# Fillers in the PSUM banks of waiting first-batch matmuls, full-width summary scores, and new transfer times in a static schedule

## The chip, the cores and the metric

The kernel runs on one core of one Trainium2 chip. The metric is the device time of one execution in microseconds (us), lower is better. Ratios are the mean time of one kernel's runs over the mean time of the other's runs of the same rounds, so they are not quite the ratio of the medians quoted beside them. A trace is one execution; times in a trace count from its first instruction, and its span is 1.7 to 2.1 us shorter than the device time.

Engines: PE is TensorE (matmul), PEld its weight loads, DVE VectorE, ACT ScalarE, POOL GpSimd, SP SyncE.

## The reference

A block-sparse attention (4 batches x 8 heads, 768 positions, head size 64) feeds a mixture of 8 dense experts whose weights per token come from eight rounds of row and column normalisation.

```python
k_sum = k.reshape(B, H, nb, 32, D).max(axis=3)          # nb = 24 blocks
v_sum = v.reshape(B, H, nb, 32, D).mean(axis=3)
scores_l = q k^T / 8, kept where |i - j| < 16           # local window
scores_s = q k_sum^T / 8 + log(32)                      # "summary scores"
attn = softmax([scores_l, scores_s]) @ [v, v_sum]       # -> x, 3072 x 512
P = exp(x @ w_gate - max); 8 x: normalise rows, columns
out = sum_e P[:, e] * (relu(x @ w1[e]) @ w2[e])         # F = 1024
```

## The kernel before

Two heads form a pair; there are 16 pairs, four to a batch. The first batch (pairs 0 to 3) is cut into halves of the positions so that PE can start early. Expert 0 is computed from each batch as soon as its x is there (its first matmuls are named `hps`), and its projections are `yps`. After about 130 us experts 1 to 7 follow as a multiplication scheme with seven products instead of eight (`pA`, `pQ`, `pR`, `pY`).

Every instruction belongs to a unit of work with an estimated cost. A list scheduler in the kernel's own Python simulates the engines with these costs and fixes, when the kernel is built, the order of each engine.

```python
def load(key, fn, issue, us, deps=()):          # one HBM load in the schedule
    last[0] = add("POOL", issue, fn, [last[0], *deps])
    last[1] = add("DMA", us, None, [add("RING", 0, None, [last[0]], lag=...), last[1]], 100.0)
    U[key] = add("LAND", 0, None, [last[1]], lag=0.9)
...
load(("v", i), lambda: load_v(i), 1.05, 1.85, ...)      # us: time of the transfer
load("w2", lambda: load_w2(0), 0.85, 5.0)
...
# copies of the 16 rows of v next to each chunk, into V_e ("near rows"), pairs 4 to 11
U["near", i] = add("SP", 2.4, lambda: near_values(i), [U["v", i], ...], prio, lag=3.5)
# values of a pair (named av): need near rows, among others
U["A", i, h] = add("PE", 0.4, lambda h=h: values(i, h), [..., U["near", i]], prio, opens=[buf])
...
# order of PE for the first batch, fixed by hand: T, Q transposes of k, q; v block sums;
# S local scores; s summaries; A values; t transposes to x
plan.follow("PE", "T0 Q0 v0 S0 T1 Q1 s0 S1 T2 Q2 s1 A0 S2 v1 T3 A1 Q3 s2 t0 S3 v2 t1 s3 v3 A2 A3 t2 t3")
# where the plan sees PE wait, it puts a matmul on zeros (named idle) until expert 0's first relu
plan.idle = (0.22, lambda: keep_busy(1), U["rl", 0, 0])
```

Summary scores from pair 4 on, two matmuls on 64 columns of the array, one for each half of the positions:

```python
def summaries_2(i):
    r, ss = i % NB, bank("a", "ss")
    for h in range(2):
        at["ss", i, h] = ss[64 * h:64 * h + 64]
        nc.tensor.matmul(ss[64 * h:64 * h + 64, 0:HS], lhsT=ksT[r][:, 0:64],
                         rhs=qT[r][:, W + h * HS:W + (h + 1) * HS], start=True, stop=True)
```

The softmax here doesn't subtract the row's maximum and nothing guards it: scores larger than these inputs give would overflow.

Of the kernel before, what the change touches and what calls it, by code (L numbers as in the profile page):

```python
# [10 lines left out]
BF16 = mybir.dt.bfloat16  # L11
# [117 lines left out]
def kernel(  # L129
# [10 lines left out]
    nc = tc.nc  # L140

    B, H, S, D = q.shape
# [3 lines left out]
    F = moe_w1.shape[2]  # L146
# [4 lines left out]
    PB = H // 2  # L151
    SCALE = 1.0 / float(D) ** 0.5
    W = 16
# [7 lines left out]
    X_BY_DMA = 12  # L161
    WHOLE = 12

    const = ctx.enter_context(tc.tile_pool(name="const", bufs=1))
# [58 lines left out]
    with tc.manual_schedule():  # L223
# [14 lines left out]
        ks = [attn.tile([128, 1, 32], BF16, name=f"ks{i}") for i in range(NB)]  # L238
        ksT = [attn.tile([128, 128], BF16, name=f"ksT{i}") for i in range(NB)]
        v_x = [attn.tile([128, 2, G, VD], BF16, name=f"vx{i}") for i in range(NQ)]  # L240
# [95 lines left out]
        def key_max_split(i):  # L336
            r = i % NB
            nc.vector.tensor_tensor(out=ksT[r][:, 0:64].rearrange("p (j n) -> p j n", j=2),
                                    in0=ks[r][:].to_broadcast([128, 2, 32]),
                                    in1=own[:].to_broadcast([128, 2, 32]), op=ALU.mult)  # L340
# [7 lines left out]
        def block_sums(i):  # L348
            sv = v_x[i % NQ]
            vs = at["vs", i] = bank("a", "vs")[:, 0:2 * D]  # L350
            for g in range(G):
                nc.tensor.matmul(vs.rearrange("p (j d) -> p j d", j=2), lhsT=m_blk[:, g, :],  # L352
                                 rhs=sv[:, :, g, 0:D], start=(g == 0), stop=(g == G - 1))
# [85 lines left out]
        def summaries(i, h, tag):  # L439
            r = i % NB  # L440
            ss, rhs = bank(tag, "ss"), qT[r][:, W + h * HS:W + (h + 1) * HS]
            at["ss", i, h] = ss
            if i < PB and not h:
                for j in range(2):
                    p = slice(64 * j, 64 * j + 64)
                    nc.tensor.matmul(ss[32 * j:32 * j + 32, 0:HS], lhsT=ks[r][p, 0, :], rhs=rhs[p],
                                     start=True, stop=True)
                return
            nc.tensor.matmul(ss[:, 0:HS], lhsT=ksT[r][:], rhs=rhs, start=True, stop=True)

        def summaries_2(i):
            r, ss = i % NB, bank("a", "ss")
            for h in range(2):
                at["ss", i, h] = ss[64 * h:64 * h + 64]
                nc.tensor.matmul(ss[64 * h:64 * h + 64, 0:HS], lhsT=ksT[r][:, 0:64],  # L455
                                 rhs=qT[r][:, W + h * HS:W + (h + 1) * HS], start=True, stop=True)

# [15 lines left out]
        def scores_h(i, h):  # L473
            sg = at["sg", i, h] = banks2("sg")
            for s in range(HG):
                for j in range(2):
                    score_mm(i, sg[:, j, s * LIVE:(s + 1) * LIVE], j, HG * h + s, 0, LIVE)
            for j in range(2):
                score_mm(i, sg[:, j, HG * LIVE:HG * LIVE + W], j, *((HG, 0, W), (HG - 1, LIVE - W, LIVE))[h])
# [18 lines left out]
        def values_h(i, h):  # L498
            sv, em, es = v_x[i % NQ], E_h[(PB * h + i) % NEH], at.pop(("es", i, h))
            av = at["av", i, h] = bank("a", "av")  # L500

            def mm(p0, p1, cc, j, lhsT, rhs, n=VD, start=False, stop=False):
                o = cc * 2 * VD + j * VD
                nc.tensor.matmul(av[p0:p1, o:o + n], lhsT=lhsT, rhs=rhs, start=start, stop=stop,  # L504
                                 skip_group_check=True)

            for cc in range(HG):
                for j in range(2):
                    mm(0, 128, cc, j, em[:, j, cc, 2 * W:2 * W + 128], sv[:, j, HG * h + cc, :],
                       start=(cc == 0 and j == 0))  # L510
            for cc in range(HG):
                c = HG * h + cc
                for j in range(2):
                    if c + 1 < G:
                        mm(96, 128, cc, j, em[0:32, j, cc + 1, 0:32], sv[0:32, j, c + 1, :])
                    if c > 0:
                        mm(0, 32, cc, j, em[96:128, j, cc - 1 if cc else HG, LIVE:PADL],
                           sv[96:128, j, c - 1, :])
            for cc in range(HG):
                mm(0, 128, cc, 0, es[:, cc, :], V_s[i][0:128 if h else 64], n=2 * VD, stop=True)  # L520
# [82 lines left out]

        def keep_busy(n):

            t = bank("m", "idle")
            for _ in range(n):
                nc.tensor.matmul(t[:], lhsT=zeros[:, 0:128], rhs=zeros[:], start=True, stop=True)

# [7 lines left out]
        nc.vector.memset(zeros, 0.0)  # L617
        keep_busy(9)
        for t in v_x:
# [18 lines left out]
        def constants():  # L638
# [10 lines left out]
            for t in ksT:  # L649
                nc.vector.memset(t[:, 64:128], 0.0)  # L650
            for t, n in ((own, 64), (own_n, 32)):
# [200 lines left out]
        def load_pair(i, parts="kqv"):  # L852
            old = i - NQ
            for c in parts:
                if c == "v":
                    load(("v", i), lambda: load_v(i), 1.05, 1.85,
                         [U.get(("A", old, 1)), U.get(("near", old))])
                elif i < PB and c in "qr":
                    h = "qr".index(c)
                    load(("q", i, h), lambda h=h: load_qk(i, 1, h), 0.65, 0.65)  # L860
                else:
                    z = "kq".index(c)
                    load((c, i), lambda z=z: load_qk(i, z), 0.75 if i < PB else 1.65,
                         1.2 if i < PB else 1.55, [U.get(("tr", old, z)), U.get(("tr", old, 2))])

        def pair_start(i, prio):
# [9 lines left out]
            for z in range(0 if i >= BY_DMA else 1 if i < PB else 2):  # L876
                buf = Buffer("m" if i < PB else "a")
                U["tr", i, z] = add("PE", 0.5 if i < PB else 0.34, lambda z=z: tr(i, z),
                                    [U["kq"[z], i], U["ident"]] + (war_k, war_q)[z]
                                    + [U["tr", i, 0] if z else ahead], prio, opens=[buf])  # L880
                U["kT", i, z] = add({"ACT": 0.8, "DVE": 0.95 if i < PB else 0.56}, 0,
                                    lambda z=z: tr_out(U["kT", i, z].on, i, z), [U["tr", i, z]], prio,
                                    uses=[buf])
            U["ks", i] = add("DVE", 0.95, lambda: key_max(i), [U["kT", i, 0], U.get(("km", o))], prio)
            if i >= PB:
                U["km", i] = add("DVE", 0.23, lambda: key_max_split(i), [U["ks", i]] + war_q[2:], prio)
            buf = Buffer("a")
            U["vs", i] = add("PE", 0.4, lambda: block_sums(i),
                             [U["v", i]] + ([U.get(("A", i - NE, 1)), U["vc", i % NE]] if i >= PB else []), prio + 0.01, opens=[buf])
# [39 lines left out]
        def pair_whole(i, prio):  # L929
# [17 lines left out]
            for h in range(2):  # L947
# [4 lines left out]
            buf = Buffer("a")  # L952
            U["ss", i, 0] = U["ss", i, 1] = add("PE", 0.22, lambda: summaries_2(i),
                                                [U["km", i], U["kT", i, 1], U.get(("A", i - NE, 1))], prio, opens=[buf])
# [66 lines left out]
        U["k", 0] = add({"ACT": 0.8}, 0, cast_k, [U["kf32"]])  # L1021
        U["vf32"] = add("LAND", 0, None, [add("RING", 0, None, [])], lag=5.6)
        U["v", 0] = add({"DVE": 0.6}, 0,
                        lambda: copy(U["v", 0].on, v_x[0][:, :, :, 0:D], v_f32), [U["vf32"]])
        U["ident"] = last[0] = add("POOL", 0.35, ident_constant, [last[0]])
        load_pair(1, "kq")
        U["band"] = last[0] = add("POOL", 0.7, band_constants, [last[0]])
        load_pair(2, "kq")
        load_pair(1, "v")
        load_pair(3, "kq")  # L1030
        load_pair(2, "v")
        load_pair(3, "v")
        for n in range(4):
            load(("w1", n), lambda n=n: load_w1(0, n, 4), 0.85, 1.25)
            if n == 1:
                for i in range(PB):
                    load_pair(i, "r")
        load_pair(PB, "kq")
        load("w2", lambda: load_w2(0), 0.85, 5.0)
        for n in range(NE):  # L1040
# [3 lines left out]
        for i in range(PB):  # L1044
# [8 lines left out]
                 "A": lambda i: U["A", i, 0], "n": lambda i: U["no", i, 0], "t": lambda i: U["xt", i, 0],  # L1053
                 "x": lambda i: U["x", i, 0]}
        plan.follow("PE", [first[c[0]](int(c[1])) for c in
                           "T0 Q0 v0 S0 T1 Q1 s0 S1 T2 Q2 s1 A0 S2 v1 T3 A1 Q3 s2 t0 S3 v2 t1 s3 v3 A2 A3 t2 t3".split()])
        plan.follow("DVE", [first[c[0]](int(c[1])) for c in
# [209 lines left out]
        experts()  # L1267
        plan.idle = (0.22, lambda: keep_busy(1), U["rl", 0, 0])
        for u in plan.order():
# [32 lines left out]
```

## Time and profile before

| | before |
|---|---|
| first three runs | 668.05, 667.20, 670.12 us |
| span in the trace | 666.5 us |
| PE busy | 99% |
| first fast clock of PE | 10.21 us |
| first values (`av`) / first hidden matmul (`hps`) | 12.81 / 19.95 us |

From the page of the kernel before, part 1 (busy us, share of the span, instructions) and part 4 (the chain that ended last):

```profile
PE 658.6 (99%) x5130; PEld 435.5 (65%) x5131; DVE 546.8 (82%) x1030; ACT 414.9 (62%) x773; POOL 198.2 (30%) x256
...
PE 97%; DMA 1%; DVE 1%; issue 0%; ACT 0%; POOLq 0%; DVEq 0%
```

PE bounds the kernel, so time can only come from making PE's work shorter or from the places where PE does nothing useful. Those are in the first 20 us. The timeline of PE before (start us, us, engine, line, operation, out<-in, count, and in brackets the idle time before it and what ended it):

```profile
1.27 4.02 PE L608 MATMUL idle<-zeros 128*128 128x512 bf16 x9 [1.27 <-DVE zeros L617]
5.26 0.85 PE L297 MATMUL tkq<-ident,kst 128*64 128x128 bf16 x12
6.76 0.53 PE L309 MATMUL tkq<-ident,qst 64*64 64x64 bf16 x12 [0.65 <-DMA qst<-in_q_dram]
7.22 0.61 PE L608 MATMUL idle<-zeros 128*128 128x512 bf16 x1
7.63 0.85 PE L352 MATMUL vs<-vx,m_blk 128*128 128x128 bf16 x6
8.27 0.63 PE L608 MATMUL idle<-zeros 128*128 128x512 bf16 x1
8.83 0.59 PE L344 MATMUL sg<-qT,kT 64*128 64x160 bf16 x8
...
17.75 0.81 PE L608 MATMUL idle<-zeros 128*128 128x512 bf16 x3
18.49 0.34 PE L446 MATMUL ss<-qT,ks 64*32 64x384 bf16 x2
...
19.95 0.66 PE L208 MATMUL hps<-xT,w 128*128 128x384 f16 x3
```

Read start to start, not durations: six block sums (`vs`) take 0.64 us at 7.63, but 0.35 us at 17.23, so PE ran at half clock until some time between. The trace's clock records put the switch at 10.21 us. (Views that print the granted clock show 1.00 before the first record; the spacing tells otherwise.)

Later, PE is packed.

### The profile page before, as it was taken

How to read it: one execution, taken by the hardware profiler on the slowest of the kernel's cores; microseconds unless marked ns; L12 is line 12 of the kernel's file. 1: busy time of each engine (PE TensorE's matmuls, PEld its weight loads, DVE VectorE, ACT ScalarE, POOL GpSimd, SP SyncE). 2: the span in 40 equal slices, each digit the busy share in tenths (PEclk: the TensorE clock that was granted, in tenths of full speed). 3: DMA queues.
4: the chain of work that ended last, by engine and by line, in shares of the span. 5: the costliest groups of instructions: out<-in, count | busy, mean ns of one | idle time of the engine just before them, and what ended most of it. 6: DMA issues, size and time to landing. Idle time of an engine off the chain costs nothing.

```text
span 666.5 us, 13243 instructions
## 1 busy us (share of the span) xinstructions
PE 658.6 (99%) x5130; PEld 435.5 (65%) x5131; DVE 546.8 (82%) x1030; ACT 414.9 (62%) x773; POOL 198.2 (30%) x256
## 2 busy tenths in 40 slices
PE   8999999999999999999999999999999999999996
PEld 4666655655676666666666666666666666666665
DVE  7888968799988787887789887888778877988776
ACT  5677776565886566556565665656665656555652
POOL 8899622100122222222222222222122212222123
PEclk9999999999999999999999999999999999999999
DMA  9999951800764747473654756373837465334656
GB/s 167 173 146 142 142 77 31 139 0 2 132 106 76 121 69 118 79 126 65 99 102 69 128 84 107 64 127 64 127 64 131 76 95 95 64 64 112 159 135 198
DMA packets 112542, 67.89 MB, mean 102 GB/s; under 512 B 77920, under 2 KB 90464, under 8 KB 112480
## 3 DMA queue, kind: packets, MB, share of 16 engines
q0 software_dynamic: 94800, 57.46, 65.0%
q1 hardware_dynamic: 17152, 9.58, 5.8%
q8 instruction: 40, 0.66, 0.4%
q14 instruction: 22, 0.18, 0.1%
q10 hardware_dynamic: 528, 0.02, 0.0%
HBM read 52.45 MB, written 6.29 MB: 88 GB/s over the span
## 4 chain that ended last, share of the span: by engine, by line
PE 97%; DMA 1%; DVE 1%; issue 0%; ACT 0%; POOLq 0%; DVEq 0%
PE yps L800 22%; PE pA L749 22%; PE pY L800 17%; PE pQ L749 11%; PE hps L208 6%; PE yps L213 6%; PE pR L749 5%; PE sg L344 1%; PE vs L352 1%; PE tkq L300 1%; PE av L504 1%; DMA qst<-in_q_dram 1%; PE av L430 1%; PE tx L542 1%; PE av L436 1%; PE ss L455 1%
## 5 line engine op out<-in xcount | busy, mean ns | idle before, releaser
L800 PEld LDWEIGHTS <-h 128*128 128x128 f16 x2352 | 230.1, 98 | 89.1 <-issue 1.0
L828 POOL DMA_DIRECT2D out_acc<-y x120 | 101.4, 886 | 373.0 <-ACT y L824 99.8
L824 ACT ACTIVATE y<-pY,P_sb 128x256 f32<-128x256 f32 x168 | 80.1, 478 | 124.0 <-PE pY L800 122.3
L815 DVE SCALAR_TENSOR_TENSOR out_acc<-yps,P_sb,out_acc 128x512 f32<-128x512 f32 x128 | 95.1, 744 | 29.4 <-PE yps L800 29.4
L783 DVE TENSOR_TENSOR h<-h 128x1024 f16<-128x1024 f16 x168 | 109.1, 684 | 1.4
L800 PE MATMUL pY<-w,h 128*128 128x256 f16 x672 | 100.0, 273 | 0.6 <-ACT y L824 0.6
L800 PE MATMUL yps<-w2sum,h 128*128 128x256 f16 x672 | 98.4, 273 | 0.0
L749 PE MATMUL pA<-xT,w 128*128 128x512 f16 x336 | 98.3, 379 | 0.0
L800 PE MATMUL yps<-w,h 128*128 128x256 f16 x672 | 93.1, 273 | 0.0
L815 DVE SCALAR_TENSOR_TENSOR out_acc<-pY,P_sb,out_acc 128x512 f32<-128x512 f32 x84 | 62.9, 748 | 31.6 <-PE pY L800 30.1
L749 PEld LDWEIGHTS <-w 128*128 128x128 f16 x672 | 65.8, 98 | 31.5 <-issue 0.2
L749 PEld LDWEIGHTS <-w1sum 128*128 128x128 f16 x504 | 49.3, 98 | 44.3
L771 DVE CUSTOM_DVE_ANT_0 h<-pQ,snap 128x512 f16<-128x512 f32 x84 | 57.6, 686 | 6.1 <-ACT snap L204 3.6
L771 DVE CUSTOM_DVE_ANT_0 h<-pA,snap 128x512 f16<-128x512 f32 x84 | 57.4, 683 | 5.5 <-PE pA L749 5.2
L199 ACT ACTIVATE h<-pA 128x512 f16<-128x512 f32 x84 | 50.6, 603 | 13.0 <-PE pA L749 12.9
L199 ACT ACTIVATE h<-pR 128x512 f16<-128x512 f32 x84 | 50.1, 597 | 8.6 <-PE pR L749 8.0
L204 ACT COPY pR<-pA 128x512 f32<-128x512 f32 x83 | 47.4, 571 | 7.0 <-PE pA L749 6.0
L800 PE MATMUL pY<-w2sum,h 128*128 128x256 f16 x336 | 50.4, 273 | 0.0
L749 PE MATMUL pA<-xsum,w 128*128 128x512 f16 x168 | 50.0, 379 | 0.0
L749 PE MATMUL pQ<-xT,w1sum 128*128 128x512 f16 x168 | 50.0, 379 | 0.0
L749 PE MATMUL pR<-xT,w 128*128 128x512 f16 x168 | 50.0, 379 | 0.0
L749 PE MATMUL pA<-xsum,w1sum 128*128 128x512 f16 x168 | 50.0, 379 | 0.0
(147 smaller groups left out, 852.1 us busy)
## 6 DMA issues: line engine op xcount, KB each, us to landing
out_acc<-y POOLq DMA_DIRECT2D x120, 256.0 KB, 3.4
w<-in_moe_w_dram POOLq DMA_DIRECT2D x15, 1024.0 KB, 10.1
out_dram<-out_acc SPq DMA_DIRECT2D x24, 256.0 KB, 2.5
qst<-in_q_dram POOLq DMA_DIRECT2D x32, 96.0 KB, 5.4
vx<-in_v_dram POOLq DMA_DIRECT2D x15, 192.0 KB, 6.2
kst<-in_k_dram POOLq DMA_DIRECT2D x24, 96.0 KB, 5.7
w<-in_moe_w_dram POOLq DMA_DIRECT2D x4, 256.0 KB, 7.4
kst<-in_k_dram POOLq DMA_DIRECT2D x3, 192.0 KB, 4.7
```

Source lines behind the costliest of these rows:

```text
L199: nc.scalar.activation(out=out, in_=in_, func=AF.Relu, bias=0.0, scale=1.0)
L204: (nc.scalar.copy if eng == "ACT" else nc.vector.tensor_copy)(out=out, in_=in_)
L208: nc.tensor.matmul(hp[:, 0:n], lhsT=w1s[e][:, dk, f * 128:(f + 1) * 128], rhs=xT[:, dk, t0:t0 + n], start=(dk == 0), stop=(dk == KD - 1))
L213: nc.tensor.matmul(yp[:, d], lhsT=h[:, f, c * 128:(c + 1) * 128], rhs=w2s[e][:, f, d], start=(f == 0), stop=(f == KF - 1))
L300: nc.tensor.transpose(t[:, g * 128:(g + 1) * 128], st[:, g, :, :].rearrange("p j d -> p (j d)"), ident)
L749: nc.tensor.matmul(dst[:], lhsT=lhsT, rhs=rhs, start=first and k == 0, stop=k == HK - 1, skip_group_check=True)
L771: nc.vector._custom_dve(dve_ops.TENSOR_ADD_SAT, out=ring(e, p, q)[:, q % 2, blk, :], in0=at[src, e, p, q][:], in1=at.pop(("snap", n, e, p, ...
L783: nc.vector.tensor_tensor(out=h[:, :, out_, :], in0=h[:, :, a, :], in1=h[:, :, b, :], op=op)
L800: nc.tensor.matmul(dst[:, d], lhsT=lhsT, rhs=rhs, start=f == 0 and n in (1, 5, 2), stop=f == HF - 1, skip_group_check=True)
L815: nc.vector.scalar_tensor_tensor(out=o, in0=y, scalar=scalar, in1=o, op0=ALU.mult, op1=ALU.add)
L824: nc.scalar.activation(out=at[key][:, d], in_=src, func=AF.Copy, bias=0.0, scale=P_sb[:, t, e:e + 1])
L828: nc.gpsimd.dma_start(out=o, in_=at.pop(("y", e, p, c, key))[:], accum_op=ALU.add)
```

## The change

It has three intents. PE should reach and keep its full clock in the first batch (in before it came at 10.21 us): a filler of 512 + 256 columns (F0) goes between the first k and the first q transposes, and 512-column fillers go into the PSUM bank (the buffer for the result) of a block sum, score group or summary just before it, where the matmul is thought to wait for data. Summaries of pairs 4 to 15 use all 128 columns, the second accumulating onto the first with zeros in the other half, so that no pair of 64-column matmuls stands between the full-width ones: in the trace of before 11 of the 12 pairs start 0.148 to 0.159 us after their predecessor, the two full-width summaries behind values 0.057 after theirs. And the schedule gets transfer times meant to be closer to what the loads take. The core of the diff, with cuts:

```diff
+    FILL = {"v0": 1, "S0": 1, "s0": 2, "s1": 1, "s2": 1, "s3": 3}
...
-        ksT = [attn.tile([128, 128], BF16, name=f"ksT{i}") for i in range(NB)]
+        ksT = [attn.tile([128, 192], BF16, name=f"ksT{i}") for i in range(NB)]
...
-                nc.tensor.matmul(ss[64 * h:64 * h + 64, 0:HS], lhsT=ksT[r][:, 0:64],
-                                 rhs=qT[r][:, W + h * HS:W + (h + 1) * HS], start=True, stop=True)
+                nc.tensor.matmul(ss[:, 0:HS], lhsT=ksT[r][:, 64 - 64 * h:192 - 64 * h],
+                                 rhs=qT[r][:, W + h * HS:W + (h + 1) * HS], start=h == 0, stop=h == 1)
...
+        def wait_busy(what, i, h, t):     # called at the head of block_sums, summaries, scores_h
+            for _ in range(FILL.get(what + str(i), 0) if i < PB and not h else 0):
+                stream(t, 512)
...
-                    load(("v", i), lambda: load_v(i), 1.05, 1.85,
+                    load(("v", i), lambda: load_v(i), 1.05, {1: 1.85, 4: 2.9}.get(i, 1.5),
...
-                    load(("q", i, h), lambda h=h: load_qk(i, 1, h), 0.65, 0.65)
+                    load(("q", i, h), lambda h=h: load_qk(i, 1, h), 0.65, 2.65 if i + h == 0 else 0.42)
...
-                         1.2 if i < PB else 1.55, [U.get(("tr", old, z)), U.get(("tr", old, 2))])
+                         0.95 if i < PB else 1.75 if i == PB else 1.38, [U.get(("tr", old, z)), U.get(("tr", old, 2))])
...
-        load("w2", lambda: load_w2(0), 0.85, 5.0)
+        load("w2", lambda: load_w2(0), 0.85, 4.4)
...
-            U["ss", i, 0] = U["ss", i, 1] = add("PE", 0.22, lambda: summaries_2(i),
+            U["ss", i, 0] = U["ss", i, 1] = add("PE", 0.33, lambda: summaries_2(i),
...
+        U["fill"] = add("PE", 0.64, lambda: keep_busy(512, 256), [], 0, opens=[Buffer("m")])
-                           "T0 Q0 v0 S0 ...
+                           "T0 F0 Q0 v0 S0 ...
```

Left out: wider memsets of `ksT`, costs of the first pair's units, a w1 quarter counted as 1.3 instead of 1.25 us, the landing of the first v counted 0.8 us later, and a rewrite of the list of loads that keeps their order.

More of the change, by code (lines that the diff above doesn't have):

```diff
@@ L337, in key_max_split @@
             r = i % NB
-            nc.vector.tensor_tensor(out=ksT[r][:, 0:64].rearrange("p (j n) -> p j n", j=2),
+            nc.vector.tensor_tensor(out=ksT[r][:, 64:128].rearrange("p (j n) -> p j n", j=2),
                                     in0=ks[r][:].to_broadcast([128, 2, 32]),
@@ L349, in block_sums @@
             sv = v_x[i % NQ]
-            vs = at["vs", i] = bank("a", "vs")[:, 0:2 * D]
+            vs = bank("a", "vs")
+            wait_busy("v", i, 0, vs)
+            vs = at["vs", i] = vs[:, 0:2 * D]
             for g in range(G):
@@ L441, in summaries @@
             ss, rhs = bank(tag, "ss"), qT[r][:, W + h * HS:W + (h + 1) * HS]
+            wait_busy("s", i, h, ss)
             at["ss", i, h] = ss
@@ L448, in summaries @@
                 return
-            nc.tensor.matmul(ss[:, 0:HS], lhsT=ksT[r][:], rhs=rhs, start=True, stop=True)
+            nc.tensor.matmul(ss[:, 0:HS], lhsT=ksT[r][:, 64:192], rhs=rhs, start=True, stop=True)
         def summaries_2(i):
@@ L474, in scores_h @@
             sg = at["sg", i, h] = banks2("sg")
+            wait_busy("S", i, h, sg[:, 0, :])
             for s in range(HG):
@@ L500, in values_h @@
             av = at["av", i, h] = bank("a", "av")
+            wait_busy("A", i, h, av)
             def mm(p0, p1, cc, j, lhsT, rhs, n=VD, start=False, stop=False):
@@ L602, in project0, with stream, keep_busy @@
             project_mm(0, at["yp", key, c], at["h", key], c, range(4 * part, 4 * part + 4))
-        def keep_busy(n):
+        def stream(t, n):
+            nc.tensor.matmul(t[:, 0:n], lhsT=zeros[:, 0:128], rhs=zeros[:, 0:n], start=True, stop=True)
+        def keep_busy(*cols):
             t = bank("m", "idle")
-            for _ in range(n):
-                nc.tensor.matmul(t[:], lhsT=zeros[:, 0:128], rhs=zeros[:], start=True, stop=True)
+            for n in cols:
+                stream(t, n)
+        def wait_busy(what, i, h, t):
+            for _ in range(FILL.get(what + str(i), 0) if i < PB and not h else 0):
+                stream(t, 512)
         kv_f32 = hpool.tile([128, 2, 2, G, D], FP32, tag="h", name="kvf32")
@@ L617 @@
         nc.vector.memset(zeros, 0.0)
-        keep_busy(9)
+        keep_busy(*9 * [512])
         for t in v_x:
@@ L649, in constants @@
             for t in ksT:
-                nc.vector.memset(t[:, 64:128], 0.0)
+                nc.vector.memset(t[:], 0.0)
             for t, n in ((own, 64), (own_n, 32)):
@@ L877, in pair_start @@
                 buf = Buffer("m" if i < PB else "a")
-                U["tr", i, z] = add("PE", 0.5 if i < PB else 0.34, lambda z=z: tr(i, z),
+                U["tr", i, z] = add("PE", 0.65 if i == 0 else 0.5 if i < PB else 0.34, lambda z=z: tr(i, z),
                                     [U["kq"[z], i], U["ident"]] + (war_k, war_q)[z]
@@ L887, in pair_start @@
             buf = Buffer("a")
-            U["vs", i] = add("PE", 0.4, lambda: block_sums(i),
+            U["vs", i] = add("PE", 0.65 if i == 0 else 0.4, lambda: block_sums(i),
                              [U["v", i]] + ([U.get(("A", i - NE, 1)), U["vc", i % NE]] if i >= PB else []), prio + 0.01, opens=[buf])
@@ L1021 @@
         U["k", 0] = add({"ACT": 0.8}, 0, cast_k, [U["kf32"]])
-        U["vf32"] = add("LAND", 0, None, [add("RING", 0, None, [])], lag=5.6)
+        U["vf32"] = add("LAND", 0, None, [add("RING", 0, None, [])], lag=6.4)
         U["v", 0] = add({"DVE": 0.6}, 0,
@@ L1025 @@
         U["ident"] = last[0] = add("POOL", 0.35, ident_constant, [last[0]])
-        load_pair(1, "kq")
-        U["band"] = last[0] = add("POOL", 0.7, band_constants, [last[0]])
-        load_pair(2, "kq")
-        load_pair(1, "v")
-        load_pair(3, "kq")
-        load_pair(2, "v")
-        load_pair(3, "v")
-        for n in range(4):
-            load(("w1", n), lambda n=n: load_w1(0, n, 4), 0.85, 1.25)
-            if n == 1:
-                for i in range(PB):
-                    load_pair(i, "r")
+        for c in "k1 q1 b0 k2 q2 v1 k3 q3 v2 v3 w0 w1 r0 r1 r2 r3 w2 w3".split():
+            i = int(c[1])
+            if c == "b0":
+                U["band"] = last[0] = add("POOL", 0.7, band_constants, [last[0]])
+            elif c[0] == "w":
+                load(("w1", i), lambda i=i: load_w1(0, i, 4), 0.85, 1.3)
+            else:
+                load_pair(i, c[0])
         load_pair(PB, "kq")
-        load("w2", lambda: load_w2(0), 0.85, 5.0)
+        load("w2", lambda: load_w2(0), 0.85, 4.4)
         for n in range(NE):
@@ L1054 @@
                  "x": lambda i: U["x", i, 0]}
+        U["fill"] = add("PE", 0.64, lambda: keep_busy(512, 256), [], 0, opens=[Buffer("m")])
+        U["fill"].opens[0].users.append(U["fill"])
+        first["F"] = lambda i: U["fill"]
         plan.follow("PE", [first[c[0]](int(c[1])) for c in
-                           "T0 Q0 v0 S0 T1 Q1 s0 S1 T2 Q2 s1 A0 S2 v1 T3 A1 Q3 s2 t0 S3 v2 t1 s3 v3 A2 A3 t2 t3".split()])
+                           "T0 F0 Q0 v0 S0 T1 Q1 s0 S1 T2 Q2 s1 A0 S2 v1 T3 A1 Q3 s2 t0 S3 v2 t1 s3 v3 A2 A3 t2 t3".split()])
         plan.follow("DVE", [first[c[0]](int(c[1])) for c in
@@ L1267 @@
         experts()
-        plan.idle = (0.22, lambda: keep_busy(1), U["rl", 0, 0])
+        plan.idle = (0.22, lambda: keep_busy(512), U["rl", 0, 0])
         for u in plan.order():
```

## The prediction

> **What bounds the kernel now.** TensorE. The page gives PE 658.6 us busy of 666.5 (99%); the chain of waits is 97% PE. Apart from the tail, PE lacks work only in the first 20 us. There the timeline of PE shows 0.65 us of waiting for the first q transfer (until 6.76), 0.47 us before the second score group (11.26), 0.16 us at 15.01, and six scheduled idle matmuls after the opening nine: at 7.22 and 8.27 (0.43 us each), 16.75 and 17.9 (0.22 and 0.65 us). From 18.5 us on PE is packed.
>
> The early PE is also slow. The opening 512-column fillers start every 0.43 us, later ones every 0.22 us. Twelve k transposes took 0.78 us at 9.36 and 0.46 at 11.58; six block sums 0.64 at 7.63 and 0.35 at 17.23. The switch to fast lies at 10.2 us. [...]
>
> **What the change does.**
> 1. F0 puts 0.64 us of fillers (cold estimate) into that gap. Other fillers go directly before block sums, scores and summaries; they replace the scheduler's idle matmuls. If the clock is fast by 6.8, block sums, their fillers and the first scores end about 0.85 us earlier, the second k transposes another 0.3. DVE then starts the second k copy (10.25 now) about 1.1 us earlier, and with it the key maxima, the first mask (12.11) and the first values (12.81). The transfers allow this: the first w1 quarters land at 17.9 and 19.9. If the clock is still slow at 6.8, nothing is won: the same fillers stand there already. [...] I count about 0.7 of 1.1 us: 0.8 us.
> 2. Full-width summaries, 12 pairs in the packed stage. Now each pair of 64-column matmuls starts 0.15 us after its predecessor (0.057 between full-width ones) and the next starts 0.286 later: 0.436. Full width, from the four that exist: 0.057 + 2 x 0.163 = 0.383, or 0.427 after scores. Eight save 0.053, four 0.018: 0.5 us, all on the critical path. [...]
> 3. New costs in the schedule reorder work between 20 and 120 us. PE has no idle there; I give this 0 +- 0.5 us. The larger memset lies in slack of DVE.
>
> **Prediction.** 668.05 - 0.8 - 0.5 = 666.75, say 666.8 us; range 665.3 to 668.4. Faster by over 2%: 0.01; within 2%: 0.985; slower: 0.005. The runs before spread over 2.9 us, so part of the difference is noise.
>
> **What would show it.** Step 1: PE's wait before the first q transposes shrinks to under 0.15 us; 512-column fillers start every 0.22 us before 8 us; the first mask starts near 11.0 instead of 12.1; expert hidden matmuls start near 19 instead of 19.95. Step 2: summaries are 128 columns wide, 0.33 us from first to next, without the 0.15 before. From 130 us to the end the length stays within 0.3 us.
>
> **What would make it wrong.** The clock does not turn fast earlier; the fillers delay data that had already come; an earlier pipeline runs into the w1 or second-half q landings (20.2 to 22.3 us); the reordered schedule opens a gap.

"That gap" in step 1 is the wait of 0.65 us for the first q transfer, until 6.76. That fillers there bring the clock forward, and the share of 0.7, were the author's estimate, without a measurement behind them. The 1.1 us is worked out from start-to-start times of before (among them 0.64 against 0.35 us for six block sums, 0.78 against 0.46 for twelve k transposes), the 0.64 us of F0 from the 0.43 us that 512 columns took at first. As to the slack of DVE in step 3, the trace of before shows it idle for 1.01 us before 6.94.

## More of the kernel before

Around 42 us the values of pair 4 run when their near rows have come:

```profile
41.99 0.38 PE L344 MATMUL sg<-qT,kT 64*128 64x160 bf16 x6
42.30 0.36 PE L430 MATMUL av<-vx,em 128*128 128x65 bf16 x6
42.49 0.34 PE L436 MATMUL av<-Ve,Ee 128*128 128x130 bf16 x3
```

and the view by windows (us from the span's start, length, busy us of each engine with instructions, granted clock, DMA share, GB/s) shows a full PE at full clock:

```profile
41.06:44.48 3.42, 3.42 (x39) 1.69 (x39) 1.79 (x7) 2.62 (x5) 2.71 (x4) 1.00 2.68 140
44.48:47.89 3.41, 3.41 (x48) 2.66 (x47) 3.29 (x8) 2.53 (x5) 3.41 (x5) 1.00 2.40 145
```

## The result, and the profile after

| | before | after |
|---|---|---|
| median of 6 runs, same rounds | 668.53 us (667.2 to 670.5) | 669.43 us (668.61 to 671.37) |
| ratio, 95% interval | | 1.0013 (0.9991 to 1.0035) |
| span in the trace | 666.5 us | 669.6 us |
| first fast clock | 10.21 us | 6.93 us |
| first values / first hidden matmul | 12.81 / 19.95 us | 11.90 / 20.00 us |

The prediction was 666.8 us with an upper end of 668.4. The page of the kernel after has new names in the chain: DMA and POOL.

```profile
PE 661.9 (99%) x5141; PEld 437.5 (65%) x5141; DVE 549.2 (82%) x1037; ACT 411.1 (61%) x766; POOL 198.3 (30%) x256
...
PE 93%; DMA 3%; POOL 2%; SPq 0%; issue 0%; DVE 0%; ACT 0%; POOLq 0%; DVEq 0%
```

The same stretch of PE's timeline after:

```profile
5.32 0.85 PE L298 MATMUL tkq<-ident,kst 128*64 128x128 bf16 x12
6.10 1.10 PE L611 MATMUL idle<-zeros 128*128 128x512 bf16 x3
7.13 0.38 PE L310 MATMUL tkq<-ident,qst 64*64 64x64 bf16 x12
7.44 0.39 PE L611 MATMUL vs<-zeros 128*128 128x512 bf16 x1
7.67 0.51 PE L355 MATMUL vs<-vx,m_blk 128*128 128x128 bf16 x6
8.01 0.38 PE L611 MATMUL sg<-zeros 128*128 128x512 bf16 x1
8.32 0.39 PE L345 MATMUL sg<-qT,kT 64*128 64x160 bf16 x8
...
17.16 0.81 PE L611 MATMUL idle<-zeros 128*128 128x512 bf16 x3
17.80 0.81 PE L611 MATMUL ss<-zeros 128*128 128x512 bf16 x3
18.54 0.34 PE L450 MATMUL ss<-qT,ks 64*32 64x384 bf16 x2
...
20.00 0.66 PE L209 MATMUL hps<-xT,w 128*128 128x384 f16 x3
```

The clock came early as hoped (block sums 0.34 us), the first values 0.9 us earlier; and then it is gone: the last summaries start at 18.54 against 18.49 us. Six fillers stand before them, three of the scheduler's own and three new ones. The data were there long before. The keys' maxima of pair 3, from the timeline of DVE after, end at 17.42:

```profile
16.48 0.94 DVE L333 TENSOR_REDUCE ks<-kT 128x24 bf16<-128x768 bf16 x1
```

Then, at 41 us, PE waits. Before, the list of waits of PE from 20 to 125 us was empty (it leaves out pauses under 0.15 us). The timeline after, and the same list (engine, line, waited for: us in total, times, longest):

```profile
40.86 0.35 PE L433 MATMUL av<-vx,em 128*128 128x65 bf16 x6
42.46 0.43 PE L439 MATMUL av<-Ve,Ee 128*128 128x130 bf16 x3 [1.25 <-DMA Ve<-vx]
```
```profile
PE av L439 <- DMA Ve<-vx: 1.3, 1, 1.3
```

And the windows after show what followed the wait in this execution, half the clock for the next 3.41 us:

```profile
41.06:44.48 3.42, 2.17 (x49) 1.60 (x46) 2.62 (x7) 1.47 (x3) 3.42 (x5) 1.00 2.26 148
44.48:47.89 3.41, 3.41 (x23) 1.96 (x22) 0.61 (x2) 1.77 (x5) 3.41 (x5) 0.50 2.29 151
```

PE is 3.41 us busy in both kernels' second window, but with 23 matmuls instead of 48: busy time hides a slow clock. At the 101st `pA` matmul of the trace after is 3.12 us behind before, and both traces take 452.6 us from there to the end. So the whole difference lies before 217 us.

### The profile page after: what moved, and what is told of

The parts are those of the page before. It is cut to its first block, busy times and chain, and to the rows that moved or that the text cites. A ratio compares the mean times of both kernels' runs of the same rounds, so it can differ in the third digit from the quotient of the medians.

```text
span 669.6 us, 13270 instructions
## 1 busy us (share of the span) xinstructions
PE 661.9 (99%) x5141; PEld 437.5 (65%) x5141; DVE 549.2 (82%) x1037; ACT 411.1 (61%) x766; POOL 198.3 (30%) x256
## 4 chain that ended last, share of the span: by engine, by line
PE 93%; DMA 3%; POOL 2%; SPq 0%; issue 0%; DVE 0%; ACT 0%; POOLq 0%; DVEq 0%
PE yps L813 22%; PE pA L762 22%; PE pY L813 16%; PE pQ L762 11%; PE yps L214 6%; PE hps L209 6%; PE pR L762 5%; DMA w<-in_moe_w_dram 1%; DMA vx<-in_v_dram 1%; PE sg L345 1%; DMA Ve<-vx 1%; PE tkq L301 1%; PE av L439 1%; PE av L433 1%; PE ss L459 1%; PE vs L355 1%
## 5 line engine op out<-in xcount | busy, mean ns | idle before, releaser
L762 PE MATMUL pQ<-xsum,w1sum 128*128 128x512 f16 x168 | 50.0, 379 | 0.0
```

The costliest lines, as they stand in the source:

```text
L762: nc.tensor.matmul(dst[:], lhsT=lhsT, rhs=rhs, start=first and k == 0, stop=k == HK - 1, skip_group_check=True)
```

## The experiments

Because start, middle and end turned out to add up, each trace is read in two distances: from the first q transposes to the first hidden matmul ("start"), and from the first hidden matmul to the 101st `pA` matmul ("middle", called the hundredth in the expectations). The rest is 452.6 us in every run but e15_again (452.7). Each distance is that of one execution. Batches of experiments ran on different chips (e1 to e4 on one, e5 to e8 and e10 to e15 on two others), each beside 11 runs of before, so medians of different batches are compared with care. Only e4_s3 and the first set of e5_near_nofill have an interval that leaves out 1.

| run | start us | middle us | PE wait at about 40 us | fast clock from | six runs: median (range) |
|---|---|---|---|---|---|
| before | 13.19 | 194.02 | none | 10.21 | see below |
| after | 12.87 | 197.09 | 1.25 | 6.93, half 44.48 to 47.89 | 669.43 (668.61 to 671.37) |
| e1_width | 16.83 | 193.66 | none | 4.60, half 8.01 to 21.67 | 668.35 (667.02 to 671.68) |
| e2_times | 11.93 | 196.11 | 1.55 | 4.76 | 669.11 (668.23 to 672.05) |
| e3b_near | 13.10 | 193.74 | none | 4.50 | 668.33 (668.23 to 669.99) |
| e4_s3 | 12.58 | 197.58 | 1.76 | 7.09, half 44.63 to 48.05 | 670.75 (668.72 to 671.88) |
| e5_near_nofill | 11.80 | 193.76 | none | 5.46 | 666.91 (666.75 to 667.21) |
| e6_near_early | 12.01 | 194.87 | 0.94 (for v) | 4.73 | 668.28 (667.10 to 671.51) |
| e7_fill_only | 13.19 | 194.02 | none | 6.67 | 668.58 (668.49 to 672.38) |
| e8_w2 | 12.92 | 193.72 | none | 6.54 | 668.00 (667.93 to 669.26) |
| e10_gap_only | 12.01 | 194.01 | none | 5.75 | 667.24 (667.16 to 668.82) |
| e11_gap_width | 12.01 | 193.66 | none | 5.15 | 667.16 (666.84 to 671.73) |
| e12_noidle | 11.52 | 193.75 | none | 5.66 | 667.30 (666.56 to 671.06) |
| e15_again | 11.84 | 193.75 | none | 7.03 | 667.22 (666.76 to 668.36) |

The kernel before ran 33 times beside these: 12 runs from 667.15 to 667.95, 13 from 668.2 to 669.34, and 8 from 670.88 to 673.54 us. Seven of the last eight have a mean granted clock of 0.986 to 0.992; the 12 lowest have 0.999 or 1.0.

The theories. **A**: the loss comes from the new transfer times, which put the values of pair 4 ahead of the landing of their near rows. **B** (rival): fillers and wider matmuls cost packed PE time, the wait is chance. **C**: fillers inside the first batch hold work whose data had come. **D** (rival): transfers, namely the second w1 quarter, cap the start anyway. **E** (rival): the fillers cost nothing since PE waits there. **F**: the filler in the gap alone makes the clock safe. **G** (rival): the other fillers are needed too.

### e1_width: full-width summaries alone

Edit: from the kernel before, the `ksT` and `summaries_2` lines of the diff; their cost in the schedule stays 0.22, so every engine keeps its order.

> Kernel before with full-width summaries only; the order of every engine is that of before. Theory A (the loss comes from the new transfer times, which put the values of pair 4 ahead of the landing of its neighbour rows): no PE wait over 0.15 us between 20 and 120 us, time 0 to 0.5 us below before. Theory B (the wider summaries and fillers cost packed PE time): 0.5 us or more above before. From the two traces: eight pairs save 0.052 us each, four pairs after scores lose 0.05 (0.497 against 0.445), so the first product of expert 1 starts 0.2 us earlier than in before (130.6), 130.4.

Measured: 668.35 against 668.20 us, ratio 1.0009 (0.9981 to 1.0037). The middle is 193.66 against 194.02, so 0.36 us shorter; no wait: B falls for the summaries. By start-to-start times, eight pairs went from 0.436 to 0.382 and four after scores from 0.445 to 0.497, 0.2 us in sum; the other 0.1 is not traced to a place. The same pair in before and in this run:

```profile
42.85 0.34 PE L436 MATMUL av<-Ve,Ee 128*128 128x130 bf16 x3
43.12 0.35 PE L455 MATMUL ss<-qT,ksT 128*64 128x384 bf16 x2
43.40 1.04 PE L213 MATMUL yps<-w,h 128*128 128x512 f16 x4
...
46.69 0.34 PE L436 MATMUL av<-Ve,Ee 128*128 128x130 bf16 x3
46.86 0.49 PE L455 MATMUL ss<-qT,ksT 128*128 128x384 bf16 x2
47.19 1.03 PE L213 MATMUL yps<-w,h 128*128 128x512 f16 x4
```

The saving is small because the old pair ran side by side: its second matmul starts 0.003 us after the first, and the next work 0.283 us later. The full-width matmuls run one after the other, 0.162 us each. So the edit saves 0.09 us before the pair (0.150 against 0.059) and 0.12 after it (0.283 against 0.162), and pays 0.16 for the second matmul, which no longer runs beside the first.

The first `pA` came at 134.0, not 130.4, because of the clock, which runs of before lose too. In this execution the clock became fast at 4.60, and fell to half at 8.01 for 13.65 us (the spacing agrees: six block sums take 0.62 us at 20.49 and 0.35 at 22.56). The windows of this run:

```profile
4.60:8.01 3.41, 1.96 (x33) 1.07 (x32) 1.90 (x16) 1.85 (x3) 3.41 (x6) 1.00 1.32 204
8.01:11.43 3.42, 3.25 (x47) 1.95 (x43) 2.07 (x4) 1.91 (x3) 3.42 (x5) 0.50 1.58 159
11.43:14.84 3.41, 3.41 (x59) 2.52 (x53) 2.54 (x7) 2.15 (x3) 2.96 (x5) 0.50 2.11 160
...
18.25:21.67 3.42, 3.42 (x37) 2.29 (x37) 1.97 (x4) 1.96 (x3) 1.68 (x3) 0.50 1.47 189
21.67:25.08 3.41, 3.41 (x52) 2.10 (x51) 2.23 (x7) 0.48 (x1) 3.32 (x5) 1.00 1.89 133
```

In the first of these PE was busy for only 1.96 of 3.41 us; 1.17 us of the rest is the wait for the first q tile. The first hidden matmul came at 23.75 us instead of 19.95. Two of the six runs have a mean clock of 0.99 and 671.6 us, as the upper cluster of the kernel before: half clock for 13.65 of 667 us makes a mean of 0.990 (an estimate; no slow run of before was traced). That the wait caused the fall is not shown. Such a fall is the accident that the filler in the gap is meant to prevent.

### e2_times: the new transfer times alone

Edit: from the kernel before, the `load` lines of the diff for v, q, k and w2, nothing else.

> Kernel before with the new transfer times in the schedule only: no new fillers, old summaries, old PE costs. Theory A: the values of pair 4 again stand before the third part of the projections and PE waits 0.8 to 1.8 us there at about 41 us for the neighbour rows; the time is 0.5 to 3 us above before, the more if the clock drops to half for 3.4 us after the wait. Theory B: no such wait, time as before within 0.5 us.

Measured (the 3.4 us of half clock in the expectation are those of the trace of after, 44.48 to 47.89): 669.11 us, ratio 1.0019 (0.9992 to 1.0047). The order around the values of pair 4 is that of after, and PE waits again. From its timeline:

```profile
39.67 0.35 PE L430 MATMUL av<-vx,em 128*128 128x65 bf16 x6
41.57 0.40 PE L436 MATMUL av<-Ve,Ee 128*128 128x130 bf16 x3 [1.55 <-DMA Ve<-vx]
```

The middle is 2.09 us longer than before. A holds: the numbers of the schedule alone, without the new fillers and summaries, make the wait. (They also change the start: with the first q counted later, the schedule itself puts two idle matmuls into the gap before the first q transposes, at 5.75 us.) Here the clock did not fall after it, though two of the six runs, 671.12 and 672.05, have a mean clock of 0.996 to 0.997.

Why the schedule errs can be read by running its scheduler by itself (a plan, no measurement). For after it puts the near rows of pair 4 at 39.55 and their values at 39.97. In the trace the rows landed at 42.33 and PE was there at 41.0. Two terms are short: the first w2 is counted as 4.4 us, where 6.82 us passed from the landing before it to its own; and from the first of the copies to the last landing the plan has 2.4 + 3.5 = 5.9 us, the trace 34.82 to 42.33, so 7.5. The second error stood in the kernel before as well (33.83 to 41.89, 8.1 us), but there the larger times of the other loads covered most of it: the rows were planned at 40.75 and landed 1.14 us late, against 2.78 after. PE, planned at 40.98, came 1.32 us late itself, at 42.30, 0.4 us after the rows. That before had no wait here was in part luck.

### e3b_near: after, with one number of the schedule mended

```diff
-                               [U["v", i], U.get(("A", i - NE, 1)), U["vc", i % NE]], prio, lag=3.5)
+                               [U["v", i], U.get(("A", i - NE, 1)), U["vc", i % NE]], prio, lag=6.0)
```

> Kernel after with one number changed: the schedule's lag from the issue of the neighbour-row copies to their landing 6.0 us instead of 3.5 (7.5 to 8 us were measured from first issue to last landing, the schedule had 5.9). Values of pair 4 then stand four groups later. Theory A: no PE wait over 0.3 us near 41 us and no half clock after 10 us; the last attention logits and the first product of expert 1 come 1.2 us or more before those of after (132.9), and the time is 0.7 us or more below after. Theory B: the time is that of after within 0.3 us.

Measured: 668.33 us, ratio to before 1.0001 (0.9981 to 1.0022), so 1.1 us below the median of after (of other rounds). No wait: the values run at 43.22, behind scores, logits and projections:

```profile
43.22 0.36 PE L433 MATMUL av<-vx,em 128*128 128x65 bf16 x6
43.41 0.34 PE L439 MATMUL av<-Ve,Ee 128*128 128x130 bf16 x3
```

The middle falls from 197.09 to 193.74 us, and the first `pA` comes at 129.1 instead of 132.9. A again. Five of six runs lie within 0.3 us of each other, but 1 us above the lowest cluster of before: the start, 13.10 us at a clock that was fast from 4.50, is still no better than before's 13.19 at a slow clock.

### e4_s3: after without the three fillers before the last summaries

Edit: `"s3": 3` taken out of `FILL`; order unchanged.

> Kernel after without the three fillers before the last first-batch summaries; order unchanged. Theory C (those fillers hold data that had come at 17.4): the last summaries start at 17.9 instead of 18.54 and the first hidden matmul of expert 0 at 19.35 instead of 20.0. Rival D (the second w1 quarter, landing at 19.84, holds the third hidden group): the first hidden matmul comes early but PE waits about 0.3 to 0.5 us for the third one, so the first 22 us gain at most 0.3 us. In both the wait at 41 us stays 1 to 2 us, and the time is within 0.7 us of after.

Measured: 670.75 us, ratio to before 1.003 (1.0007 to 1.0054). In this execution the first q tile landed 0.5 us later than in after (7.40 against 6.89), so the absolute times of the expectation (17.9, 19.35) were missed: 18.57 and 20.03. Counted from the first values, the last summaries come after 6.00 us instead of 6.64, and the first hidden matmul after 7.46 instead of 8.10: the 0.64 us of three fillers, exactly. C holds and E falls. PE did not wait for the third hidden group, but here this says nothing of D: the hidden matmuls began at 20.03, after the second w1 quarter had landed (19.77). e5_near_nofill and e12_noidle settle D: there they begin at 18.64 and 18.47, the quarter lands at 19.15 and 19.52, and PE waits for no w1. The total did not profit, and the expectation of a time within 0.7 us of after was missed (1.3 us above its median, other rounds). In the trace the wait at 41 us grew to 1.76 us because the rows landed 0.53 us later than in after (42.86 against 42.33); PE came to them at the same time. The clock was at half from 44.63 to 48.05, after the wait. Why the six runs as a whole are slower is not shown.

### e5_near_nofill and e15_again: no fillers but the one in the gap

Edit: e3b_near with `FILL = {}`. Same PE order.

> Kernel e3b_near (lag of the neighbour rows 6.0) with an empty table of fillers; the order of PE is that of e3b_near, the filler in the gap before the first q transposes stays. Theory C (the fillers inside the first batch hold work that could run, about 1 us between the first values and the first hidden matmul): that distance is 7.1 to 7.3 us instead of 8.10, and undisturbed runs lie about 0.9 us below those of e3b_near, near 667.3. Rival E (the fillers cost nothing since PE waits there anyway): distance and undisturbed time as in e3b_near. Theory F (the fillers are an insurance of the clock): one or two of six runs show a mean clock of 0.99 and lie 3 to 4 us higher; without F no such run.

Measured: 666.91 us against 668.54, ratio 0.9964 (0.993 to 0.9998); all six runs from 666.75 to 667.21. The start falls from 13.10 to 11.80 us, and the distance from the first values to the first hidden matmul from 8.10 to 7.13. The two ends of the start, e3b_near first, then e5_near_nofill:

```profile
6.97 0.38 PE L310 MATMUL tkq<-ident,qst 64*64 64x64 bf16 x12 [0.45 <-DMA qst<-in_q_dram]
20.07 0.66 PE L209 MATMUL hps<-xT,w 128*128 128x384 f16 x3
...
6.84 0.38 PE L310 MATMUL tkq<-ident,qst 64*64 64x64 bf16 x12 [0.32 <-DMA qst<-in_q_dram]
18.64 0.66 PE L209 MATMUL hps<-xT,w 128*128 128x384 f16 x3
```

The six runs lie 1.4 us below e3b_near (another chip), more than the 0.9 expected; the fillers before the first values, which the expectation left out, account for 0.33 us of the 1.30 in the traces. C holds, E falls. No run lost its clock (mean clocks 0.998 to 1.0), against the expectation of theory F as it was put then (that the fillers in `FILL` are the insurance). This is the lowest median.

> e5_near_nofill again on the same chip and rounds as the three above: six runs within 0.7 us near 666.9 and no run with a mean clock of 0.993 or less; 0.2 to 0.4 us below e10_gap_only, level with e11_gap_width within 0.3.

Measured: 667.22 us against 668.25, ratio 0.9969 (0.9936 to 1.0002); the range, 666.76 to 668.36, is wider than expected, and the median is level with e10_gap_only (667.24), not 0.2 to 0.4 us below it. So the kernel is not shown to be faster than e10_gap_only or e11_gap_width. Its trace shows 0.24 us of waiting at 16.3 for the third v tile, so some of the spread is transfers.

### e6_near_early: fillers of the first pair only

Edit: e3b_near with `FILL = {"v0": 1, "S0": 1, "s0": 2}`.

> Kernel e3b_near with the fillers of the first pair only (before the first block sums, scores and summaries), none before the summaries of pairs 1 to 3. Theory C: first values to first hidden matmul 7.1 to 7.3 us, undisturbed runs near 667.3; theory F: no run with a mean clock of 0.99, so the median beats e3b_near by 0.5 to 1 us. Rival E: as e3b_near.

Measured: 668.28 us, ratio 0.9988 (0.9953 to 1.0023), inconclusive as a time: runs spread from 667.10 to 671.51, one at a mean clock of 0.994. First values to first hidden matmul are 7.13 us, as C says. In the profiled execution PE waited 0.94 us at 39.91 for a v tile that landed at 39.87, where e3b_near with the same order had none: a late transfer of this execution.

### e7_fill_only: all the new fillers on the kernel before

Edit: before with `FILL`, `wait_busy` and F0; old transfer times, costs and summaries. The PE order differs from before by one idle matmul, replaced by F0.

> Kernel before with all the new fillers alone: old transfer times, old PE costs, old summaries; the PE order is that of before but for one idle matmul against the new gap filler. Theory C: first values to first hidden matmul 7.9 to 8.2 us against 7.14 in before; no PE wait over 0.3 us at 41 us; undisturbed runs 0.5 to 1.2 us above the lowest of before (667.2), so 667.7 to 668.4. Theory F: no run with mean clock 0.99. Rival E: undisturbed runs as before or lower.

Measured: 668.58 us against 668.54, ratio 1.0006 (0.9969 to 1.0042). Four runs within 0.13 us near 668.5, just above the 667.7 to 668.4 expected; two at 672, whose mean clock (0.997 and 0.999) does not explain them, and they were not traced. First values to first hidden matmul are 8.11 us against 7.14; the middle is that of before, 194.02. So the fillers bring the clock forward and cost as much as that wins: start 13.19 in both.

### e8_w2: after with w2 counted as 6.2 us

Edit: `load("w2", ..., 0.85, 6.2)` instead of 4.4.

> Kernel after with one number of the schedule changed: the transfer of the first w2 counted as 6.2 us instead of 4.4 (5.6 to 6.8 were measured from the landing before it to its own). The schedule then puts the values of pair 4 four groups later by itself. Theory A: no PE wait over 0.3 us near 41 us, time as e3b_near (668.3) within 0.4 us and 0.7 us or more below after. If the wait stays, the lag of the neighbour rows and not the w2 time is the number that misled the schedule.

Measured: 668.00 us, ratio 0.9983 (0.9952 to 1.0015); no wait, middle 193.72. So either number mends the order; the w2 time was wrong in itself, 5.0 to 6.8 us in the 14 traces, never 4.4.

### e10_gap_only: the filler in the gap alone

Edit: before with the `"fill"` unit and `F0` of the diff.

> Kernel before with the filler in the gap before the first q transposes and nothing else of the change (PE order of before but for one idle matmul). Theory F (it is this filler that makes the clock safe, the others only cost): no run with a mean clock of 0.993 or less, where 4 of 28 runs of before so far had one with times of 670.9 to 673.5; clock fast for good by 8.1 us in the trace; first values to first hidden matmul 7.1 to 7.3; undisturbed runs near the lowest of before, 667.2, spread under 0.7 us in most. Rival G (the other fillers are needed to hold the clock): one or two of six runs fall to 0.993 or less.

Measured: 667.24 us against 668.25, ratio 0.997 (0.9937 to 1.0002); five of six runs from 667.16 to 667.29, the lowest cluster of before. The start takes 12.01 us instead of 13.19. Its timeline shows PE waiting for data in the same places where after has fillers, at no loss:

```profile
5.97 0.50 PE L608 MATMUL idle<-zeros 128*128 128x512 bf16 x2
6.99 0.38 PE L309 MATMUL tkq<-ident,qst 64*64 64x64 bf16 x12 [0.52 <-DMA qst<-in_q_dram]
7.76 0.50 PE L352 MATMUL vs<-vx,m_blk 128*128 128x128 bf16 x6 [0.40 <-DVE vx L204]
```

So the filler makes no execution faster than the best ones of before, which reach 667.15 without it; it makes the good case the usual one (five of six runs here, 12 of 33 of before). (The "4 of 28" of the expectation is 3: the run of 673.0 us has a clock of 0.997.) F is supported: over all kernels with this filler, 3 of 66 runs have a mean clock of 0.994 or less; of those without it, 9 of 45, or 9 of 39 if e2_times, whose schedule filled the gap by itself, is left out. G is not settled: all three are among the 36 runs without the later fillers (e5, e6, e10, e11, e12, e15), none among the 30 that have them or most of them; so few runs cannot tell that from chance.

### e11_gap_width: the gap filler and full-width summaries

Edit: e10_gap_only plus the edit of e1_width.

> e10_gap_only plus full-width summaries, transfer times and PE order of before. From e1_width against before (first hidden matmul to the hundredth pA matmul 193.66 against 194.02 us): 0.36 us below e10_gap_only, so undisturbed runs near 666.8, level with e5_near_nofill. If it is as good, the new transfer times bring nothing.

Measured: 667.16 us, ratio 0.9978 (0.9936 to 1.0019). The lowest run is 0.32 us below e10_gap_only's lowest, the middle 0.35 us shorter; one run of six, 671.73 at a clock of 0.99, spoils the mean. It is level with e5_near_nofill's second set within 0.1 us, so the new transfer times, even mended, bring nothing that these runs resolve.

### e12_noidle: also without the scheduler's own idle matmuls

Edit: e5_near_nofill with `plan.idle` ending at the summaries of pair 1 instead of expert 0's first relu.

> e5_near_nofill without the scheduler's own idle matmuls from the second summaries on (five matmuls). Theory C: the last summaries start when their keys are ready, about 0.35 us earlier, and the first hidden matmul comes 0.3 to 0.4 us earlier. Theory D: the third hidden group then waits for the second w1 quarter (19.15 to 19.9), so the total gains under 0.2 us. Theory G: without these fillers the clock falls in one or two of six runs.

Measured: 667.30 us, ratio 0.998 (0.9943 to 1.0017); the lowest run of the study, 666.56, but also 669.63 and 671.06 (clock 0.988). The start falls by 0.28 us to 11.52, so C and not D; PE now waits 0.64 us for the keys' maxima. The risk to the clock cannot be judged from one such run in six.

## Why the prediction was wrong, point by point

In short: the clock came early as forecast, but two steps failed. The new fillers were counted as replacing idle matmuls and came on top of them (point 3), and the new schedule was counted as free and opened a wait (point 5).

1. *"TensorE bounds the kernel; PE lacks work only in the first 20 us."* Right.
2. *"F0 puts 0.64 us of fillers (cold estimate) into that gap ... 0.8 us."* Right: the first fast clock came at 6.93 us in the trace of after, against 10.21 before. The filler alone is worth 1.0 us in the median (667.24 against 668.25; the ratio's interval, 0.9937 to 1.0002, just includes no gain), where 0.8 was estimated. That the trace of before had a late clock was chance: e1_width, with the same order of PE, had it at 4.60 us. What sets the moment of the switch is not shown: the first fast clocks of the 14 traces lie anywhere from 4.50 to 10.21 us.
3. *"Other fillers ... replace the scheduler's idle matmuls."* Wrong; the first step that failed. They came on top: 17 fillers after the opening nine, against six before, and six of the 17 are still the scheduler's own. In the first batch they cost 1.3 us: start 13.10 with them, 11.80 without (e3b_near, e5_near_nofill), medians 668.58 and 667.24 (e7_fill_only, e10_gap_only). The prediction listed "the fillers delay data that had already come" as a risk but put no number on it. The intermediate signs it named came true (first mask at 11.07 against "near 11.0"; the wait before the first q transposes under 0.15), but hidden matmuls near 19 did not: 20.00.
4. *"Full width: 0.5 us, all on the critical path."* A gain, but its size is off: 0.36 us in the trace. The term that was mis-sized is the pair after scores: 0.427 us was taken from a score group that ends in 16-column matmuls, but behind a 160-column one the first full-width matmul starts 0.162 after its predecessor, the second 0.172 after the first and the next work 0.163 later, 0.497 in all, so these four lose 0.05 each. Behind values, from predecessor to start, it is 0.150 us with the 64-column pair and 0.059 with the full-width one, as counted on; why is not shown. The gain is small because the old pair ran side by side (see e1_width).
5. *"New costs reorder work ...; PE has no idle there; I give this 0 +- 0.5 us."* Wrong; the step that cost most. That PE had no idle showed only that the old order was right for the old times. The reorder opened a wait of 1.25 us, start to start 1.60 instead of 0.18, so 1.42 us lost. In the profiled run half clock followed for 3.41 us, at most 1.7 us of loss (half of 3.41, an estimate); of the six runs of after only this one has a mean clock as low as 0.997. That the wait caused the fall is not shown: in e2_times a longer one left the clock alone. The sum for the middle: 1.42 + 1.70 - 0.36 = 2.76; measured 3.07, and 0.3 stays unexplained. The new order has other neighbours, and the distances in point 4 differ by neighbour (0.162 behind scores, 0.059 behind values); what that is worth was not tested.
6. *"From 130 us to the end the length stays within 0.3 us."* Right only from the 101st `pA` on (452.6 us both); at 130 us different amounts of expert 0's work were left.

In medians: -1.0 (gap filler), +1.3 (other fillers), -0.1 to -0.4 (width), +1.1 (order; after less e3b_near, other rounds) makes 1.0 to 1.3 us slower, and 0.9 was measured. Each step of this size is under 0.2% and comes from a few runs; the traces' distances are the firmer ground.

## What to carry to other kernels

A filler paid here where the engine was certain to wait, one gap in front of a transfer (1.0 us in the median, e10_gap_only), and cost its full length where it stood in order before work whose data may have come (0.64 us for three, e4_s3): check the end of the producer against the start of the filler. In a statically scheduled kernel, estimates are a set: mending some and not others can uncover an error that the old ones covered, so after a change of costs compare the planned and the measured time of every landing and look for new waits of the bounding engine. When runs of one kernel fall in clusters, find the clusters' cause (here, for the slowest one, the clock: a mean of 0.986 to 0.992 in seven of eight runs, 0.999 or 1.0 in the fastest 12) before comparing medians, and compare distances between the same two instructions in the traces.

## What the traces show of the clock, and what they leave open

- Besides the drop at the kernel's end (665.57 us in before, 669.12 in after), the three falls traced lasted 3.41 us (after), 3.42 (e4_s3) and 13.65 (e1_width). The 3.41 us before the fall held 1.25 us of wait in after, and 1.45 us without PE work in e1_width, 1.17 of them one wait. In e4_s3 the clock fell after a wait of 1.76 us, in e2_times it did not after 1.55. So the length of a wait alone does not tell these cases apart.
- In e1_width PE was busy for 3.25, 3.41, 3.08 and 3.42 of 3.41 or 3.42 us in four stretches in a row at half clock; only after the fourth was the clock full again. So the busy time of a stretch does not tell when the clock returns either. What does is not shown.
- Next to a 64-column pair the start-to-start distances are longer: about 0.09 us before it (0.150 against 0.059) and 0.12 after it (0.283 against 0.162).
